# ScalarE instead of SyncE issues the exchange of the transposed exponentials, and VectorE makes two of the output copies

## The chip, the cores and the metric

The kernel runs on one core of a Trainium2 chip. A core has TensorE (PE: matrix products, with its weight load, PEld), VectorE (DVE), ScalarE (ACT), GpSimd (POOL) and SyncE (SP), and 16 DMA engines. The engines run side by side and wait for each other through semaphores. The metric is the time of one execution on the device, in microseconds (us).

## The reference

Three stages follow each other, all in float32.

```python
# 1: attention in chunks of 64 positions, 32 heads-by-batch, head size 64
scores = scale * np.matmul(q_c, k_c.transpose(0, 1, 2, 4, 3))
attn = np.exp(scores - np.max(scores, axis=-1, keepdims=True))
attn = attn / (np.sum(attn, axis=-1, keepdims=True) + 1e-09)
x = np.matmul(attn, v_c)                      # as (2304 tokens, 512)
# 2: eight experts, all of them on every token, weighted by P
P = np.exp(x @ w_gate - max); eight rounds of row and column norms
for e in range(E):
    out += P[:, e:e + 1] * (np.maximum(x @ w1[e], 0.0) @ w2[e])
# 3: a maximum of three products, then one more product
h = np.maximum(np.maximum(x @ w1, x @ w2), x @ w3)
return h @ w_out
```

## The kernel before

The 2304 tokens are 18 tiles of 128, in three blocks of six tiles. An expert has a hidden size of 1024, and a pair of hidden tiles (256 columns) is the unit of the main loop, so an expert is four pairs and all experts are 32 pairs. The loop counter `n` runs over items: 0 to 31 are the pairs of block 0, 32 to 63 those of block 1, 64 to 95 those of block 2, and the rest is stage 3. In this text "pass n" is one turn of this loop.

In each pass `up(n)` computes the pair's hidden values with seven half-size products in place of eight (product positions 0 to 6, line L353). The products of the banks `pa`, `pg` and `pb` build upon each other in PSUM: ScalarE copies the first three to `s` (L360), VectorE adds them to later ones (L366), and the relus (L298) and low parts (L304, L301) follow. The fifth product's sum, `c<-pa`, has to be read out of its bank before product 6 is accumulated into that bank. Between the positions stand the down products of the pair before (`down`, L469), two at each of the positions 1, 3 and 5. They go to two buffers, `dn`, and are taken out by `evict`: for the first pair of an expert by a copy of ScalarE (L482), for the other three by an addition of VectorE (L484, later L488). Since it is the pair before that is evicted, ScalarE does this in the passes 1, 5, 9 and so on.

The values are split in a high part (a cast by ScalarE, L272 in `hilo`, also L159 and L203) and a low part (a subtraction by GpSimd, L273, or VectorE). In block 0 the weights are prepared in the same way while they are used: `prep` and `prep_x` take `sw`, ScalarE copies a part to `xw` in PSUM (L188), VectorE computes four sums from it (L193 to L197), ScalarE casts (L203), VectorE subtracts (L210). `keep` stores the prepared weights for the later blocks (L216 to L223).

The attention of tiles 6 to 17 is spread over the same passes, 1 to 12, one tile each. At position 0 come the scores (`s<-qk`, L804), the gate's product (L922), the value product of the tile before (`xp<-aT,v`, L905, into the `dn` buffers too), the exponentials (L838), at position 1 the norm and VectorE's transposition of 32 by 32 blocks into `eT` (L865), and at position 2 `att_swap`: ScalarE copies `eT` to `aT` (L872), and four transfers of 32 KB inside SBUF then exchange the blocks that have to change partitions (L876). `aT` has two buffers, and `xp` of the next pass reads it.

All engines work through their instructions in the order in which the code above emits them; there is no scheduler that changes it. All transfers are issued by SyncE, in that order too, so that an issue that waits holds up those after it. A transfer tells of its landing by one of a few semaphores.

After block 0's last pair, `y_out` brings its finished tiles into the other layout: four transpositions by TensorE into `yp` (L506), a copy by ScalarE back to `ar` (L508), a store. The last two tiles are done together in pass 34, position 0.

Of the kernel before, what the change touches and what calls it, by code (L numbers as in the profile page):

```python
# [33 lines left out]
NPAIR = E * F // 256  # L34
# [18 lines left out]
def kernel(ctx: ExitStack, tc: tile.TileContext, qk, vv, wg, wts, wts2, out):  # L53
    nc = tc.nc
# [445 lines left out]

    y_due = []

    def y_out(t):
        p = wk.tile([P, KD, P], F32, name="yp", tag="wk")
        for k in range(KD):
            nc.tensor.transpose(p[:, k], ar[:, t, k * P:(k + 1) * P], ident)  # L506
        y = ar[:, t].rearrange("p (k q) -> p k q", k=KD)
        nc.scalar.copy(out=y, in_=p)  # L508
        nc.sync.dma_start(out=ys[t], in_=y)

    def fold_all():
# [270 lines left out]
    def load_qk(t):  # L782
        if t >= NT:
            return
        a = q_t[t] = ap_.tile([P, KD, 2, P], F32, name="qk", tag="qk", bufs=3)
        if t < 3:
            nc.sync.dma_start(out=a[:, 0:2], in_=qk[t, :, 0:2])
            nc.sync.dma_start(out=a[:, 2:4], in_=qk[t, :, 2:4])
        else:
            nc.sync.dma_start(out=a, in_=qk[t])  # L790

    def load_v(t):
        if t < NT:
            v_t[t] = ap_.tile([P, DM], F32, name="v", tag="v", bufs=3)
            nc.sync.dma_start(out=v_t[t], in_=vv[t])
# [72 lines left out]
    def att_swap(t):  # L868
        eT = et_t.pop(t)
        aT = ap_.tile([P, 2, H, 32], F32, name="aT", tag="aT")  # L870
        at_t[t] = aT
        nc.scalar.copy(out=aT, in_=eT)  # L872
        for c in range(2):
            for i in range(2):
                src, dst = 64 * c + 32 * i, 64 * c + 32 * (1 - i)
                nc.sync.dma_start(out=aT[dst:dst + 32, i], in_=eT[src:src + 32, 1 - i])  # L876

    def raw_of(t):
        if t // 2 not in raw_t:
# [124 lines left out]
    for m in range(NT - NPE):  # L1004
        t, n = NPE + m, 1 + m
# [5 lines left out]
    n = NT - NPE + 2  # L1011
# [80 lines left out]
    for k in (4, 5):  # L1092
        for j in range(TS // 2):
            n = first_of[k - 1] + 3 * j
            if k == 4 and j < 2:
                n = first_of[3] + 3 + j
# [17 lines left out]
    with tc.manual_schedule():  # L1114
        nc.vector.memset(wones, 1.0)
        load_qk(0)
        load_qk(1)
        load_v(0)
        load_qk(2)
        raw1(1)  # L1120
        nc.vector.memset(wgr, 0.0)
        nc.vector.memset(ones, 1.0)
        nc.scalar.activation(out=first, in_=ones[:, 0:8], func=AF.Exp)
        make_identity(nc, ident)
        warm(13)
        scores = lambda t: att_qk(t, [head_s(t)[:, g] for g in range(2)])
        scores(0)
        load_qk(3)
        load_v(1)
        part = [plain(j, f)[0] for j in range(3) for f in range(2)]  # L1130
        half_of = lambda i, q: part[i](slice(q, q + 1))
        for k in range(NPE + 2):
            if k == 4:
                half_of(0, 0)
            if k + 1 < NPE:
                warm(4 if k < 4 else 0)
                scores(k + 1)
                if k < 2:
                    load_qk(k + 4)
            if k < NPE:  # L1140
                head_exp(k)
            if k in (1, 2):
                prep(1, k - 1)
            if k >= 5:
                half_of(*((0, 1), (1, 0), (2, 1))[k - 5])
            if k >= 2:
                att_pv(k - 2)
                load_v(k + 1)
            if k == 0:
                load_v(2)  # L1150
            if k == 1:
                raw1(0)
                raw2(0)
                warm(6)
            if k == 4:
                nc.sync.dma_start(out=wgr[:, :, 0:E], in_=wg)
            if k == 5:
                half_of(2, 0)
            if k >= 5:
                load_qk(k + 1)  # L1160
            if 1 <= k <= NPE:
                head_norm(k - 1)
                att_T(k - 1)
            if k == 3:
                xg = x_cols(0, raw_t[0], nc.gpsimd, ap_, xh, xl)
                next(xg)
            if k == 4:
                next(xg)
                next(xg)
            if k == 5:  # L1170
                xg = x_mid(1, raw_t[1])
            if k in (5, 6):
                next(xg)
        part[3]()
        half_of(1, 1)
        part[4]()
        part[5]()
        keep(1, 0)
        raw1(2)
        next(xg)  # L1180
        w2 = w2_first()
        xg = x_last(2, raw_t[2])
        for _ in range(3):
            next(xg)
        next(xg)
        ends = [[plain(j, f)[1:] for f in range(2)] for j in range(3)]
        for j in range(3):
            if j == 2:
                for _ in range(3):
                    next(w2)  # L1190
            for i in range(2):
                for end in ends[j]:
                    end[i]()
        prep_x(0, 0)
        prep_x(0, 1)
        raw2(1)
        prep_sums(2)
        prep_x(0, 2)
        prep_x(0, 3)
        hps.close()  # L1200
        psum = lambda name, n: pool(name, n, space=bass.MemoryType.PSUM, reuse_waits="tile")
        wk, ps_a, dn, ps_g, ps_b = psum("wk", 2), psum("pa", 2), psum("dn", 2), psum("pg", 1), psum("pb", 1)

        pend = [(0, q, j) for q in (1, 0) for j in range(TS // 2)]
        for n in range(1, ni):
            it = items[n]
            big_m = it["kind"] == "m"
            raw1(n + 2)
            for pos in up(n):
                clock[0] = 7 * n + pos  # L1210
                if y_due and y_due[0][0] < 7 * n + pos - 1 and (len(y_due) > 2 or n != NPAIR + 1):
                    y_out(y_due.pop(0)[1])
                    if (n, pos) == (NPAIR + 2, 0):
                        y_out(y_due.pop(0)[1])
                if (n, pos) in early:
                    early[n, pos]()
                if pos in ((2, 4) if n == 1 else (0, 1)):
                    prep(n + 1, pos // 2 - 1 if n == 1 else pos)
                if pos == 2:
                    prep(n, 2)  # L1220
                    prep_x(n, 0)
                elif pos == 5 + (n == 1):
                    prep_x(n, 3)
                for f in bg.get((n, pos), ()):
                    f()
                if (n, pos) != (NPAIR + 1, 6):
                    step()
                if pos < 3:
                    decode_step(n)
                if n <= NPAIR:  # L1230
                    run = 2 if pos in (1, 3, 5) else 0
                else:
                    run = len(pend) if pos == 6 and big_m and it["i"] == 0 else 0
                    if run and n > ni - 4:
                        run = 4
                for i in range(run):
                    if pend:
                        down(*pend.pop(0))
                    while pos == 5 and later:
                        later.pop(0)()  # L1240
                    if n in xcol and n != first_of[3] + 4 and i in (0, 2, 4):
                        next(xcol[n])
                    if (n, i) == (first_of[3] + 3, 3):
                        x_next(4, 1, n + 1)
                if run and big_m and not pend:
                    room(4)
                if pos == 3 + (n == 1):
                    prep_x(n, 1)
                    prep_x(n, 2)
                    raw2(n + 1)  # L1250
            if NPAIR + 2 <= n < first_of[3] + 2:
                for i in half((n - NPAIR) // 2 - 1, n % 2):
                    if n + 1 in first_of[2:4]:
                        if i in (3, 5):
                            x_put((i + 3) // 2, 0)
                    if i in (1, 3):
                        decode_step(n)
                    step()
                while n % 2 == 0 and extras:
                    step()  # L1260
            if n + 1 == first_of[3] + 2:
                while extras:
                    step()
                big_again()
            if it["down"] and (n < NPAIR or big_m):
                assert len(pend) == (2 if n == ni - 1 else 0)
                pend += [(n, q, j) for q in (1, 0) for j in range(TS // 2)]
        while later:
            later.pop(0)()
        for d in pend:  # L1270
            down(*d)
        assert not chunks
# [38 lines left out]
```

## Time and profile before

| | |
|---|---|
| median of 3 runs | 1775.23 us (1775.12 to 1779.2) |
| the profiled execution | 1775.73 us, span 1774.0 us |
| TensorE busy | 1763.7 us (99% of the span) |
| TensorE's weight load busy | 1684.0 us (95%) |
| VectorE busy | 1297.2 us (73%) |
| GpSimd busy | 994.4 us (56%) |
| ScalarE busy | 776.6 us (44%) |
| granted TensorE clock | 1.00 in the whole span (2.4 GHz) |
| DMA | 532.89 MB, mean 300 GB/s, one hardware queue with 83.2% of the engines' span |

The span goes from the first to the last instruction; the execution's own time is a little longer. Busy times don't count register, semaphore and DMA-issuing instructions, so ScalarE's and SyncE's issues are not in them. A row of the timeline has a start, a duration (both us), the engine, the line of the kernel, the operation, out<-in with its shape, and a count where several of a kind are merged; in brackets stand the engine's idle time before it and what ended it. SPq marks SyncE's issues.

### The profile page before, as it was taken

How to read it: one execution, taken by the hardware profiler on the slowest of the kernel's cores; microseconds unless marked ns; L12 is line 12 of the kernel's file. 1: busy time of each engine (PE TensorE's matmuls, PEld its weight loads, DVE VectorE, ACT ScalarE, POOL GpSimd, SP SyncE). 2: the span in 40 equal slices, each digit the busy share in tenths (PEclk: the TensorE clock that was granted, in tenths of full speed). 3: DMA queues.
4: the chain of work that ended last, by engine and by line, in shares of the span. 5: the costliest groups of instructions: out<-in, count | busy, mean ns of one | idle time of the engine just before them, and what ended most of it. 6: DMA issues, size and time to landing. Idle time of an engine off the chain costs nothing.

```text
span 1774.0 us, 30179 instructions
## 1 busy us (share of the span) xinstructions
PE 1763.7 (99%) x10768; PEld 1684.0 (95%) x10768; DVE 1297.2 (73%) x2342; ACT 776.6 (44%) x1566; POOL 994.4 (56%) x891
## 2 busy tenths in 40 slices
PE   9999999999999999999999999999999999999999
PEld 7888888999989999999999999999999999999998
DVE  8767667678876688887886887878787766664535
ACT  6665664655555534343333434434333333323221
POOL 4665665777777766666675677576767555000000
PEclk9999999999999999999999999999999999999999
DMA  8999987899988897988888779888888786877662
GB/s 287 332 349 359 368 322 299 324 374 343 354 306 336 325 321 272 337 298 306 277 316 305 268 256 347 305 297 296 319 301 314 264 306 243 282 258 255 243 245 107
DMA packets 206486, 532.89 MB, mean 300 GB/s; under 512 B 16160, under 2 KB 95360, under 8 KB 181248
## 3 DMA queue, kind: packets, MB, share of 16 engines
q1 hardware_dynamic: 206336, 530.97, 83.2%
q8 instruction: 85, 1.39, 0.3%
q14 instruction: 65, 0.53, 0.1%
HBM read 373.31 MB, written 156.02 MB: 298 GB/s over the span
## 4 chain that ended last, share of the span: by engine, by line
PE 95%; DMA 2%; DVE 1%; ACT 1%; issue 0%; POOL 0%; SPq 0%; DVEq 0%; ACTq 0%; POOLq 0%
PE pa L353 28%; PE dn L411 27%; PE dn L469 18%; PE pg L353 14%; PE pb L353 7%; DMA aT<-eT 1%; DMA upart<-ar 0%; PE xp L905 0%; DMA w2s<-w2y 0%; PE s L804 0%; DMA sw<-in_wts 0%; PE gp L922 0%; PE hq L1112 0%; PE hs L804 0%; DVE e L830 0%
## 5 line engine op out<-in xcount | busy, mean ns | idle before, releaser
L353 PE MATMUL pa<-xh,wr 128*128 128x384 f32 x1808 | 529.6, 337 | 0.7 <-ACT s L360 0.6
L469 PE MATMUL dn<-wr,hr 128*128 128x512 f32 x1476 | 356.2, 392 | 0.0
L353 PEld LDWEIGHTS pa<-xh,wr 128*128 128x128 f32 x1808 | 332.7, 188 | 7.1 <-ACT s L360 1.3
L469 PEld LDWEIGHTS dn<-wr,hr 128*128 128x128 f32 x1476 | 275.4, 188 | 53.9
L353 PE MATMUL pa<-xl,wr 128*128 128x384 f32 x904 | 303.2, 335 | 0.0
L411 PE MATMUL dn<-hr,wr 128*128 128x384 f32 x1344 | 274.7, 335 | 0.0
L353 PE MATMUL pg<-xh,wr 128*128 128x384 f32 x904 | 268.3, 337 | 0.0
L360 ACT COPY s<-pa 128x384 f32<-128x384 f32 x244 | 117.3, 481 | 301.0 <-PE pa L353 278.3
L411 PEld LDWEIGHTS dn<-hr,wr 128*128 128x128 f32 x1344 | 237.0, 188 | 0.0
L366 DVE TENSOR_TENSOR c<-pb,s 128x384 f32<-128x384 f32 x82 | 45.7, 557 | 203.0 <-PE pb L353 179.5
L273 POOL TENSOR_TENSOR hr<-c,hr 128x384 fp32r<-128x384 f32 x96 | 111.0, 1161 | 145.3 <-ACT hr L272 139.0
L411 PE MATMUL dn<-hx,wr 128*128 128x384 f32 x840 | 182.8, 338 | 0.0
L353 PEld LDWEIGHTS pa<-xl,wr 128*128 128x128 f32 x904 | 169.7, 188 | 4.0
L353 PEld LDWEIGHTS pg<-xh,wr 128*128 128x128 f32 x904 | 166.4, 188 | 1.6 <-issue 0.4
L353 PE MATMUL pg<-xl,wr 128*128 128x384 f32 x452 | 151.1, 334 | 0.0
L411 PEld LDWEIGHTS dn<-hx,wr 128*128 128x128 f32 x840 | 150.9, 188 | 0.0
L273 POOL TENSOR_TENSOR hr<-tq,hr 128x384 fp32r<-128x384 f32 x128 | 148.2, 1173 | 0.1
L353 PE MATMUL pb<-xh,wr 128*128 128x384 f32 x452 | 134.1, 337 | 0.0
L420 DVE TENSOR_TENSOR ar<-dn,ar 128x384 f32<-128x384 f32 x240 | 122.9, 546 | 9.3 <-PE dn L411 8.9
L273 POOL TENSOR_TENSOR hx<-c,hx 128x384 fp32r<-128x384 f32 x60 | 68.4, 1143 | 106.5 <-ACT hx L272 106.2
L411 PE MATMUL dn<-hy,wr 128*128 128x384 f32 x504 | 111.1, 336 | 0.0
L420 DVE TENSOR_TENSOR ax<-dn,ax 128x384 f32<-128x384 f32 x180 | 93.1, 549 | 18.5 <-PE dn L411 18.5
(246 smaller groups left out, 3207.7 us busy)
## 6 DMA issues: line engine op xcount, KB each, us to landing
wr<-w2s SPq DMA_DIRECT2D x80, 1024.0 KB, 6.1
w1s<-wr SPq DMA_DIRECT2D x32, 1792.0 KB, 10.5
wr<-w1s SPq DMA_DIRECT2D x53, 1024.0 KB, 8.0
wr<-w1s SPq DMA_DIRECT2D x58, 768.0 KB, 6.9
w2s<-wr SPq DMA_DIRECT2D x55, 512.0 KB, 5.4
wr<-w2s SPq DMA_DIRECT2D x52, 512.0 KB, 7.1
wr<-scr SPq DMA_DIRECT2D x22, 1024.0 KB, 5.1
wr<-scr SPq DMA_DIRECT2D x27, 768.0 KB, 6.1
```

The lines of the kernel that those rows point to most:

```text
L273: (eng or nc.gpsimd).tensor_tensor(out=l, in0=v, in1=h.bitcast(F32), op=ALU.subtract)
L353: nc.tensor.matmul(ps, lhsT=wt[:, x, ws], rhs=y[:, xi, k], start=b not in begun, stop=k == 1 and i == 2, skip_group_check=True)
L360: nc.scalar.copy(out=s[pos], in_=ps)
L366: nc.vector.tensor_tensor(out=inner, in0=ps, in1=s[other], op=ALU.add)
L411: nc.tensor.matmul(p, lhsT=w[:, a, dt * P:(dt + 1) * P], rhs=h[m][:, b], start=m == 0 and q == 0, stop=m == 1 and q == 2)
L420: nc.vector.tensor_tensor(out=o, in0=p, in1=o, op=ALU.add)
L469: nc.tensor.matmul(o, lhsT=h[:, hi, ts], rhs=w, start=(f == 0 and i == 0), stop=(f == 1 and i == 2))
```

## The change

Line L876 is issued by ScalarE's queue instead of SyncE's; the four transfers, their data and their place in the code stay. In pass 34, position 0, the two copies of `y_out` are VectorE's instead of ScalarE's; the other four tiles of block 0 keep ScalarE's copy.

```diff
-    def y_out(t):
+    def y_out(t, copy=nc.scalar.copy):
...
-        nc.scalar.copy(out=y, in_=p)
+        copy(out=y, in_=p)
         nc.sync.dma_start(out=ys[t], in_=y)
...
                 src, dst = 64 * c + 32 * i, 64 * c + 32 * (1 - i)
-                nc.sync.dma_start(out=aT[dst:dst + 32, i], in_=eT[src:src + 32, 1 - i])
+                nc.scalar.dma_start(out=aT[dst:dst + 32, i], in_=eT[src:src + 32, 1 - i])
...
                 if y_due and y_due[0][0] < 7 * n + pos - 1 and (len(y_due) > 2 or n != NPAIR + 1):
-                    y_out(y_due.pop(0)[1])
-                    if (n, pos) == (NPAIR + 2, 0):
-                        y_out(y_due.pop(0)[1])
+                    last = (n, pos) == (NPAIR + 2, 0)
+                    for _ in range(1 + last):
+                        y_out(y_due.pop(0)[1], nc.vector.tensor_copy if last else nc.scalar.copy)
```

## Rows read from the trace of the kernel before

**Rows 1.** Part 1 of the page: busy us (share of span) xinstructions.

```profile
PE 1763.7 (99%) x10768; PEld 1684.0 (95%) x10768; DVE 1297.2 (73%) x2342; ACT 776.6 (44%) x1566; POOL 994.4 (56%) x891
```

**Rows 2.** TensorE's waits over the span: us in total, times, longest.

```profile
PE xp L905 <- DMA aT<-eT: 0.8, 1, 0.8
```

**Rows 3.** Stretches: length, then busy us by engine, clock, DMA share, GB/s.

```profile
124.00:141.00 17.00, 16.08 (x114) 14.18 (x107) 12.84 (x29) 9.14 (x21) 9.37 (x9) 1.00 0.99 348
...
192.00:210.00 18.00, 17.57 (x158) 15.30 (x157) 12.27 (x28) 10.66 (x25) 10.40 (x10) 1.00 0.94 346
```

**Rows 4.** The tile aT: durations in ns min/median/max; its transfers' time to landing.

```profile
L876 SPq DMA_DIRECT2D aT<-eT x48: 507/718/1372, 44.8 to 239.8; - x48
...
DMA to landing us min/median/max: 2.8/6.5/11.3
```

**Rows 5.** Timeline of SyncE's issues, 36 to 250 us: the exchange.

```profile
44.76 2.73 SPq L876 DMA_DIRECT2D aT<-eT  x4
...
60.50 3.50 SPq L876 DMA_DIRECT2D aT<-eT  x4
...
167.44 4.85 SPq L876 DMA_DIRECT2D aT<-eT  x4
...
184.15 3.84 SPq L876 DMA_DIRECT2D aT<-eT  x4
...
202.61 4.56 SPq L876 DMA_DIRECT2D aT<-eT  x4
...
219.74 2.41 SPq L876 DMA_DIRECT2D aT<-eT  x4
```

**Rows 6.** Timeline of pass 1, 42.6 to 53 us.

```profile
42.65 0.62 ACT L872 COPY aT<-eT 128x512 f32<-128x512 f32 x1 [0.79 <-DVE eT L865]
...
43.18 0.83 ACT L272 CAST wr<-st 128x768 fp32r<-128x768 f32 x1
...
46.05 1.06 ACT L482 COPY ar<-dn 128x512 f32<-128x512 f32 x2
...
47.02 2.92 PE L469 MATMUL dn<-wr,hr 128*128 128x512 f32 x12
...
52.46 0.69 PE L804 MATMUL s<-qk 64*64 64x64 f32 x30 [0.16 <-DVE wr L210]
```

**Rows 7.** Timeline of pass 2, 60 to 68.5 us.

```profile
61.41 0.79 ACT L188 COPY xw<-sw 128x256 f32<-128x256 f32 x2
...
64.02 0.68 DVE L193 TENSOR_TENSOR wr<-xw,wr 128x512 fp32r<-128x512 f32 x1
...
66.20 0.55 DVE L366 TENSOR_TENSOR c<-pa,s 128x384 f32<-128x384 f32 x1
...
68.08 0.33 PE L353 MATMUL pa<-xh,wr 128*128 128x384 f32 x1
```

**Rows 8.** Timeline of pass 5, 110 to 128 us.

```profile
109.07 1.25 SPq L790 DMA_DIRECT2D qk<-in_qk  x1
...
113.39 3.87 SPq L876 DMA_DIRECT2D aT<-eT  x4
...
115.28 0.58 ACT L482 COPY ar<-dn 128x512 f32<-128x512 f32 x1
...
117.95 2.92 PE L469 MATMUL dn<-wr,hr 128*128 128x512 f32 x12
```

**Rows 9.** SyncE's waits, 184 to 189 us; the page's issues: KB, us to landing.

```profile
SPq L876 <- DMA qk<-in_qk: 1.1, 1, 1.1
...
qk<-in_qk SPq DMA_DIRECT2D x15, 512.0 KB, 6.7
```

**Rows 10.** Timeline of pass 34, 574 to 580 us.

```profile
575.18 1.08 ACT L508 COPY ar<-yp 128x512 f32<-128x512 f32 x2
...
578.42 0.56 DVE L366 TENSOR_TENSOR c<-pb,s 128x384 f32<-128x384 f32 x1 [1.38 <-PE pb L353]
...
578.71 0.44 PE L353 MATMUL pa<-xh,wr 128*128 128x384 f32 x1 [0.42 <-ACT s L360]
```

## The prediction

> **What bounds the kernel now.** I read the page first. TensorE is busy 1763.7 us of a span of 1774.0 us [rows 1], so in the whole program it stands idle 10.3 us. A change that only takes waits away cannot gain more than that. Then I read TensorE's list of waits and the table of stretches. The wait that the change aims at is there: the value product `xp<-aT,v` waits for the exchange `aT<-eT` once, for 0.8 us [rows 2], in the stretch from 124 to 141 us, where TensorE is idle for 0.92 us; from 192 to 210 us it loses another 0.43 us ahead of the same product [rows 3]. A third wait, of `pa` for the copy `s`, takes 0.42 us at 578.71 us [rows 10], where the two moved copies are. TensorE's other waits lie in the first 21 us, but for two of 0.2 us.
>
> So the gain has a ceiling of about 1.8 us (0.92 + 0.43 + 0.42), a tenth of a per cent. The question is what ScalarE's new work costs.
>
> **The issue moves to ScalarE.** There are 12 exchanges of 4 transfers, in passes 1 to 12 of the pair loop, with 48 issues of 0.51 to 1.37 us (median 0.72 us), landing 2.8 to 11.3 us later [rows 4]. SyncE spends 2.41 to 4.85 us on the four [rows 5], six rows of the 12. In the order of the code they now stand on ScalarE between the copy L872 and the casts L159 and L272 (in pass 1 the cast L272). ScalarE starts its next instruction 0.53 us after L872 begins, 0.09 us before L872 ends [rows 6]; now it must let L872 end, issue four transfers, and start again. Hence everything behind is late by the four issues plus some 0.2 us.
>
> What do four issues cost on ScalarE? The trace has none there, so I bound them by SyncE's. The lower end is nothing per issue. The nearest undisturbed row is pass 11, where the four take 2.41 us [rows 5]; the long ones come where large transfers of the same queue are still in flight, and ScalarE's queue would hold nothing else. I take 2.4 us, so a lateness of 2.6 us. The upper end is 4.85 + 0.2 = 5.05 us.
>
> One more thing can hold ScalarE. In pass 9 the four took 3.84 us because one waited 1.1 us for the load `qk` to land [rows 5, 9], which has nothing to do with `aT`: the semaphores that tell of a landing are used again in turn, and an issue waits until the earlier transfer on its semaphore is in. If ScalarE's issues take part in that turn, ScalarE stands still for it. In pass 5 the `qk` load leaves at 109.07 us [rows 8] and such a load needs 6.7 us [rows 9], so the last issue could not end before some 116.5 us: lateness 3.3 us. In pass 9 it is 4.0 us, in pass 1 about 2.9 us.
>
> **Who waits for the late ScalarE.** Queued behind the issues are the casts, the copies `xw` L188, the relu L298 and, in some passes, the eviction of the down product. I looked for each consumer's slack.
>
> In passes 2 to 4, 6 to 8 and 10 to 12 the evictions are VectorE's. There the chain is L188, then VectorE's L193 to L197, then L366 `c<-pa`, which frees the bank that TensorE wants at product 6. L188 ends at 62.20 us and VectorE comes to L193 at 64.02: 1.8 us of slack. L366 ends at 66.75 and TensorE begins product 6 at 68.08: 1.3 us more [rows 7]. A lateness up to 3.1 us costs nothing; mine is 2.6. Nine passes at 0.
>
> In passes 1, 5 and 9 the pair before is the first of its expert and ScalarE itself evicts `dn` (L482). There are two `dn` buffers. In pass 5 the first eviction ends at 115.86 us and TensorE wants that buffer at 117.95 [rows 8]: slack 2.1 us; pass 9 has the same pattern 70.89 us later. With lateness 2.6 us each loses 0.5 us, with the semaphores' turn 1.2 and 1.9 us.
>
> Pass 1 is the worst. ScalarE has no gap there: the first L482 is done at about 46.6 us and TensorE wants the buffer at 47.02; at the end of the pass TensorE waits 0.16 us for L210, which ends the chain through ScalarE [rows 6]. The lateness goes through nearly whole: 2.6 to 2.9 us.
>
> **What it gives back.** The exchange no longer stands behind SyncE's bulk transfers, and the two waits ahead of `xp`, 0.92 and 0.43 us [rows 3], should go: four transfers of 32 KB on a queue of their own have to land only by the next pass. The Trainium skill's DMA: Bandwidth & Descriptors (Queues, rings and completion order) says that SyncE and ScalarE each own a row of rings and that a DMA engine takes turns between rows; by that the 1.3 us are regained.
>
> SyncE is freed of a wait too: the store `xs<-xr` leaves earlier. The next, the load of `sw`, waits for VectorE anyway. I count nothing.
>
> **Two copies to VectorE.** At 575.18 us ScalarE copies two outputs in 1.08 us, and TensorE then waits 0.42 us for a late `s` at 578.71 us. VectorE has 1.38 us idle before 578.42 us [rows 10]. Two copies at ScalarE's rate fit. At half that rate (2.2 us) VectorE would be 0.8 us late. I take a gain of 0.4 us; the ends are a gain of 0.42 and a loss of 0.8 us.
>
> **The sum.** Without the semaphores' turn: 2.6 + 0.5 + 0.5 − 0.92 − 0.43 − 0.4 = +1.9 us. With it: 2.9 + 1.2 + 1.9 − 0.92 − 0.43 − 0.4 = +4.3 us. The trace shows the turn, so I lean to the second, but the loss in pass 1 gives the transfers time to catch up: +4.0 us. The profiled execution took 1775.73 us (span 1774.0 and 1.7 around it) and would take 1779.7; it lies 0.5 us above the median of 1775.23, so I forecast 1779.2 us. That is 0.23%, under the 0.3% (5.3 us) that a measurement can tell from no change.
>
> **Rivals.**
>
> *ScalarE's issues are as long as SyncE's.* Then lateness follows the 12 rows of SyncE plus 0.2 us. Of the nine easy passes three have 4.56 to 4.85 us, 1.6 to 1.9 us above the slack, 5.3 us together; the other six have 2.41 to 3.50 us [rows 5] and give some 1.1 us. Pass 1 gives 2.9, passes 5 (3.87 us [rows 8]) and 9 some 1.9 each, less 1.75 of gains: +12 us, 1787 us. It decides from a lateness of 3.1 us on, at product 6 of the VectorE passes. For it: every issue after the first in a group is longer where bulk is in flight. Against it: the other queue would be nearly empty. By the Trainium skill's Perfetto Trace Analysis (DMA Instruction — HWDGE (DVE, Sync)) the recorded issue includes a wait for a generator locked for one user at a time; that would speak for this rival. Chance 0.27.
>
> *An issue on ScalarE costs next to nothing.* Lateness is some 0.5 us: pass 1 loses 0.5 to 0.7, the rest none, and the gains stay: −1 us, 1774.2 us. Against it is that no issue on SyncE is below 0.5 us. Chance 0.13.
>
> *The exchange lands no sooner on ScalarE's queue,* so the change doesn't do what it is made for: the 1.35 us are not regained, +5.4 us, 1780.6 us. By the Trainium skill's DMA: Bandwidth & Descriptors (Issuing engines are not separate DMA queues) it would be so: all issuers share the same DMA engines, and a second one saves only the time of issuing. For it: the DMA engines are 0.99 busy from 124 to 141 us [rows 3]. Against it: 32 KB needed 2.8 us at best and 11.3 us at worst [rows 4], so most of the long landings is time spent behind other transfers of the queue. Chance 0.07.
>
> *Faster by over 5.3 us.* It would need half of all of TensorE's idle time, most of it outside these passes. Chance 0.03.
>
> **How the numbers follow.** My forecast has 0.50, with its own range of 1777 to 1780.5 us; about a tenth of it lies above 1780.6. Slower by over 0.3%: 0.24 of the first rival, 0.05 of the forecast, half of the third: 0.33. Faster 0.03. The same 0.64. The range goes from 1774 (the cheap issue) to 1787 us.
>
> **What would show it.** Right: idle TensorE of 2 to 3 us at about 47 us, released by ScalarE's L482; some of it at 118 and 189 us; no wait for `aT<-eT`; landings well below 6.5 us; no new idle time before product 6 in the other passes; the wait at 578 us gone. Wrong: issues on ScalarE under 0.2 us or over 0.8 us each, or a wait ahead of L876 on ScalarE in many passes. The forecast fails most easily at the length of an issue, which I took from another engine.

## The result, and the profile after

The changed kernel takes 1795.8 us (median of 5 runs, 1793.81 to 1798.96) against 1775.23 us before (5 runs, 1774.67 to 1779.2): a ratio of 1.0115, interval 1.0099 to 1.0131. It is 20.6 us slower, well outside the forecast range. The profiled execution took 1793.81 us with a span of 1792.0 us, 18.0 us more than before; the account below is of these 18.0 us, and what the other runs have beyond them is not split up.

First, the page's busy times, which answer to [rows 1]:

```profile
PE 1767.8 (99%) x10768; PEld 1685.7 (94%) x10768; DVE 1298.3 (72%) x2344; ACT 776.0 (43%) x1564; POOL 994.9 (56%) x891
```

TensorE has the same instructions and is busy 4.1 us longer, so some of them ran slower. The other 13.9 us are idle time. TensorE's list of waits of the changed kernel (us in total, times, longest) says where:

```profile
PE pa L353 <- DVE c L366: 8.3, 7, 2.2
PE dn L469 <- ACT ar L482: 4.2, 3, 2.3
PE pa L353 <- ACT s L360: 1.9, 2, 1.6
...
PE xp L905 <- DVE ar L484: 0.6, 1, 0.6
```

Before, neither of the first two was in the list. They are the two places for which the prediction had worked out a slack: product 6 behind `c`, and the `dn` buffer behind ScalarE's eviction. The wait of `xp` for `aT<-eT` [rows 2] is gone. Adding all of TensorE's idle time in passes 1 to 12 gives 13.5 us (8.3 + 4.2 + some 1.0 ahead of `xp`) where it was 1.5: +12.0. Pass 34 gives +1.2, the first 35 us, ahead of any changed line, +0.8, and busy time +4.1; together 18.1.

The exchange itself, the tile `aT` (durations in ns, min/median/max; time to landing), answers to [rows 4]; ACTq marks ScalarE's issues:

```profile
L876 ACTq DMA_DIRECT2D aT<-eT x48: 514/804/1762, 43.7 to 256.9; - x48
...
DMA to landing us min/median/max: 3.0/5.4/7.0
```

It lands earlier, as hoped: 7.0 us at the worst, not 11.3. But an issue on ScalarE is no shorter than it was on SyncE. The four of a pass take 2.45 to 5.08 us, 3.62 us in the mean; SyncE's took 3.56, SyncE's waits between the four included. ScalarE's list of waits from 40 to 265 us shows that time as idle ("issue" here is the four issues ahead of the cast):

```profile
ACT wr L159 <- issue: 32.0, 8, 5.2
```

Pass 7 is the worst. The chain of waits from 155 to 166 us (start, length, what) leads from the copy L872 through the issues to TensorE:

```profile
154.69 0.63 ACT aT L872
...
155.34 0.51 ACTq L876
...
155.89 1.34 ACTq L876
...
157.27 1.34 ACTq L876
...
158.66 1.76 ACTq L876
...
160.46 0.62 ACT wr L159
...
161.91 0.39 ACT xw L188
...
164.51 0.56 DVE c L366
...
165.12 1.01 PE pa L353 x2
```

L159 starts 5.77 us after L872 began, where 0.53 was usual [rows 6], so ScalarE is 5.2 us late; with 3.1 us of slack 2.1 us are left. The timeline shows 2.17, and beside it a row of pass 1:

```profile
49.77 3.00 PE L469 MATMUL dn<-wr,hr 128*128 128x512 f32 x12 [2.33 <-ACT ar L482]
...
165.12 0.69 PE L353 MATMUL pa<-xh,wr 128*128 128x384 f32 x1 [2.17 <-DVE c L366]
```

The last row holds a second loss: that product takes 0.69 us where 0.33 is usual. The table of stretches has the granted clock in the column before the last two:

```profile
160.00:164.00 4.00, 2.94 (x14) 2.09 (x12) 1.65 (x4) 2.21 (x5) 1.29 (x1) 1.00 0.48 179
...
166.00:168.00 2.00, 2.00 (x8) 2.00 (x7) 2.00 (x4) 1.54 (x4) 2.00 (x2) 0.50 0.83 247
...
227.00:229.00 2.00, 2.00 (x36) 1.56 (x39) 1.77 (x4) 0.97 (x3) 1.92 (x4) 0.50 1.02 347
```

TensorE had stood idle for 2.17 us, and in pass 10, ending at 225.1 us, for 1.89 us. After each the clock was at its lower level, 0.50 (1.2 GHz), for 3.4 us. Half of these 6.8 us is 3.4 us of the 4.1; the rest I could not place. The wait of 2.33 us in pass 1 was not followed by it (twelve products in 3.00 us; 2.92 before).

Pass 34, where VectorE makes the two copies (timeline, all engines):

```profile
593.36 1.28 DVE L508 COPY ar<-yp 128x512 f32<-128x512 f32 x2
594.56 1.26 DVE L322 TENSOR_TENSOR tq<-c 128x384 f32<-128x384 f32 x1
...
595.85 0.51 ACT L272 CAST hr<-tq 128x384 fp32r<-128x384 f32 x1 [1.58 <-DVE tq L322]
596.27 0.47 ACT L360 COPY s<-pg 128x384 f32<-128x384 f32 x1
...
598.08 0.45 PE L353 MATMUL pa<-xh,wr 128*128 128x384 f32 x1 [1.65 <-ACT s L360]
```

The copies fit VectorE's load but not its order: they stand ahead of the subtraction L322, ScalarE's cast waits for that, the copy `s` stands behind the cast, and TensorE waits 1.65 us where it waited 0.42 [rows 10].

### The profile page after: what moved, and what is told of

It reads as the page before. It is cut to its first block, busy times and chain, and to the rows that moved or that the text cites. A ratio compares the mean times of both kernels' runs of the same rounds, so it can differ in the third digit from the quotient of the medians.

```text
span 1792.0 us, 30161 instructions
## 1 busy us (share of the span) xinstructions
PE 1767.8 (99%) x10768; PEld 1685.7 (94%) x10768; DVE 1298.3 (72%) x2344; ACT 776.0 (43%) x1564; POOL 994.9 (56%) x891
## 3 DMA queue, kind: packets, MB, share of 16 engines
HBM read 373.31 MB, written 156.02 MB: 295 GB/s over the span
## 4 chain that ended last, share of the span: by engine, by line
PE 91%; DVE 2%; ACTq 2%; ACT 2%; issue 2%; DMA 1%; POOL 0%; SPq 0%; DVEq 0%; POOLq 0%
PE pa L353 27%; PE dn L411 26%; PE dn L469 16%; PE pg L353 13%; PE pb L353 6%; ACTq L876 2%; PE xp L905 0%; PE hs L660 0%; ACT aT L872 0%; ACT wr L159 0%; ACT wr L272 0%; ACT xw L188 0%; DMA v<-in_v 0%; DMA aT<-eT 0%; PE s L804 0%
## 6 DMA issues: line engine op xcount, KB each, us to landing
w1s<-wr SPq DMA_DIRECT2D x32, 1792.0 KB, 10.2
```

## The experiments

The theory after these rows: ScalarE is late by its four issues, and each pass loses what exceeds its slack. Rival causes: the lateness of something else that moved (SyncE's stores, the landing), the two copies, or an issue that is long because the two engines disturb each other.

**The exchange alone**, with the copies left on ScalarE.

```diff
-                nc.sync.dma_start(out=aT[dst:dst + 32, i], in_=eT[src:src + 32, 1 - i])
+                nc.scalar.dma_start(out=aT[dst:dst + 32, i], in_=eT[src:src + 32, 1 - i])
```

> The changed kernel with the two output copies back on ScalarE. If the issue of the exchange on ScalarE is the cause: +17 to +20 us over the kernel before, TensorE's waits in passes 1 to 12 as in the changed kernel, and the wait for `s` in pass 34 back from 1.65 to 0.4 us. If the two copies are the cause: within 2 us of the kernel before.

1794.12 us beside 1775.73: ratio 1.0101, 1.0087 to 1.0114. TensorE's waits:

```profile
PE pa L353 <- DVE c L366: 9.6, 8, 2.1
PE dn L469 <- ACT ar L482: 4.2, 3, 2.6
```

So nearly all of the loss, 18.4 us, is the exchange's.

**The copies alone.**

```diff
-                    y_out(y_due.pop(0)[1])
-                    if (n, pos) == (NPAIR + 2, 0):
-                        y_out(y_due.pop(0)[1])
+                    last = (n, pos) == (NPAIR + 2, 0)
+                    for _ in range(1 + last):
+                        y_out(y_due.pop(0)[1], nc.vector.tensor_copy if last else nc.scalar.copy)
```

> The kernel before with only the two output copies on VectorE. If the exchange is the cause: +1 to +1.5 us, all of it in pass 34, where the wait for `s` grows from 0.42 to some 1.6 us. If the copies are the cause: +17 us or more.

1776.74 us: ratio 1.0006, 0.9997 to 1.0014. The time can't tell it from before, but the list of waits repeats the row of the changed kernel:

```profile
PE pa L353 <- ACT s L360: 1.8, 2, 1.6
```

**ScalarE late, the exchange on SyncE.** If lateness is the cause, dummy work in the place of the issues must bring the same waits, with no transfer on ScalarE's queue.

```diff
-    pool("edge", side="right").tile([P, 120], F32, name="edge")
+    edge = pool("edge", side="right").tile([P, 120], F32, name="edge")
...
+        for _ in range(20):
+            nc.scalar.copy(out=edge, in_=ident[:, 0:120])
```

> The kernel before (SyncE issues the exchange), with 20 small copies on ScalarE behind each L872 that nobody reads: ScalarE is late by some 3 to 4 us, as by the four issues, while queues and semaphores stay as they were. If ScalarE's lateness alone is the cause: about 3 us in pass 1, 0.5 to 1 us ahead of product 6 in each of the nine VectorE passes, 1 to 2 us in passes 5 and 9: +9 to +16 us. If the second queue and the changed order of SyncE's transfers are the cause: 0 to +3 us.

1843.7 us: ratio 1.0389, 1.0373 to 1.0405. The copies were longer than I had estimated; ScalarE's timeline in pass 2, and TensorE's waits:

```profile
68.77 6.45 ACT L878 COPY edge<-ident 128x120 f32<-128x120 f32 x20
75.13 0.62 ACT L159 CAST wr<-sw 128x512 fp32r<-128x512 f32 x1
```

```profile
PE pa L353 <- DVE c L366: 28.5, 9, 3.3
PE dn L469 <- ACT ar L482: 14.2, 3, 6.0
```

L159 is 6.4 us late. Nine passes wait for `c` 3.2 us each, which makes the slack 3.2 us. Pass 1 waits 6.0 us and the passes 5 and 9 share 8.2, 4.1 each: slacks of 0.4 and 2.3. The same two places and no others, so lateness of ScalarE alone is enough. TensorE is busy 1785.1 us, 21 us longer; its granted clock is 0.50 after ten of these twelve waits.

**The same with 11 copies**, 3.5 us, near the mean length of the four issues.

```diff
+        for _ in range(11):
+            nc.scalar.copy(out=edge, in_=ident[:, 0:120])
```

> As e3_scalar_late with 11 copies instead of 20: by the 0.318 us that each took there, ScalarE is 3.5 us late in every pass, about the mean of the four issues on ScalarE (3.6 us). SyncE issues. If lateness beyond each pass's slack is the whole cause: 0.4 us ahead of product 6 in each of the nine VectorE passes, 1.4 us in passes 5 and 9, 3 us in pass 1: 9 us of waits, +8 to +12 us with what the clock adds; less than the changed kernel, whose issues are uneven. If the changed kernel loses by something else too: +8 us all the same here, and the difference stays open.

1788.84 us beside 1775.46: ratio 1.0078, 1.0063 to 1.0093.

```profile
PE dn L469 <- ACT ar L482: 5.6, 3, 3.1
PE pa L353 <- DVE c L366: 2.2, 9, 0.4
```

Nine waits of 0.24 us: 3.5 less 3.2, again. An even lateness of 3.5 us costs 13.4 us, more than the 8 to 12 expected: 7.8 us are these waits, and TensorE is busy 1769.0 us, 5.3 us longer than before. The exchange alone has 13.8 us of these two waits. Most of that difference is a larger mean: its four issues take 3.70 us, with the 0.2 us a lateness of 3.9. By the slacks of 3.2, 0.4 and 2.3 us an even lateness of 3.9 us would give 13.0 us. Only the last 0.8 us are left for the unevenness: what exceeds the slack counts, and what falls short gives nothing back.

**The issues later in ScalarE's order**, behind the copies L188 and the evictions, ahead of L203.

```diff
+        swaps.append((aT, eT))
...
                 if pos == 3 + (n == 1):
+                    att_issue()
                     prep_x(n, 1)
```

> ScalarE issues the exchange, but behind L188 and the eviction of position 3, just ahead of L203, where ScalarE waits some 2.5 to 3.7 us for VectorE anyway; output copies on ScalarE. If the lateness of what stands behind the issues is the cause: the waits for L482 and `c` go, +0 to +5 us (pass 1 has no gap on ScalarE, and `xp` may wait for a later landing). If the second queue itself is the cause: +15 us or more, as in the changed kernel.

1778.95 us: ratio 1.0018, 1.0008 to 1.0027. The issues (L884 in this kernel, 514/602/1382 ns) are somewhat shorter, the four 3.07 us in the mean. But in passes 4, 5, 8 and 9 they take 3.75 to 3.92 us, more than the slacks at the old place, and yet no wait for `c` or for L482 is left (`xp` is L913 here):

```profile
187.41 3.87 ACTq L884 DMA_DIRECT2D aT<-eT  x4
```

```profile
PE xp L913 <- DMA aT<-eT: 1.9, 2, 1.5
PE s L804 <- DVE wr L210: 0.7, 1, 0.7
```

The place of the issues in ScalarE's order decides, not that ScalarE issues them. The price is that the exchange starts later and `xp` waits for it.

**The large store earlier.** Why are issues long on a queue that holds nothing else? SyncE's 1.8 MB store `w1s<-wr` (L216) was still in flight in most passes of the changed kernel (KB each, median us to landing):

```profile
w1s<-wr SPq DMA_DIRECT2D x32, 1792.0 KB, 10.2
```

Here it leaves at position 4 of the pass before, with the exchange on ScalarE, and in a control with the exchange on SyncE.

```diff
-                at(g + a if g or s_ else NPAIR, b, lambda g=g, s_=s_: keep(g if g or s_ else NPAIR, s_))
+                n_, b = (g - 1, 4) if 3 <= g <= 13 and not s_ else (g + a if g or s_ else NPAIR, b)
+                at(n_, b, lambda g=g, s_=s_: keep(g if g or s_ else NPAIR, s_))
```

> ScalarE issues the exchange at its place (output copies on ScalarE); the store of the 1.8 MB of prepared weights (w1s) leaves at position 4 of the pass before, for pairs 3 to 13, instead of at position 0. If the issues are long because this store's transfer is in flight right ahead of them: the four take 2.4 to 2.8 us in passes 3 to 12, the waits for `c` go, and +4 to +8 us are left over the kernel before. If they are long for another reason (a generator shared with SyncE's issues): 3.6 us on average and +15 us or more.

> Control of e6_store_earlier: the kernel before (SyncE issues the exchange) with the same earlier store. Either theory: within 2 us of the kernel before; its two waits of 1.3 us for the exchange may go, or SyncE may stand still for GpSimd.

With ScalarE 1787.89 us (ratio 1.0076, 1.006 to 1.0092), the control 1781.11 us (1.0031, 1.0019 to 1.0043). The control was to stay within 2 us and did not: the early store makes `s<-qk` wait for L210 (3.8 us) and `xp` for L482 (2.5 us). Against its own control the exchange on ScalarE now costs 6.8 us, not 18.4. ScalarE's issues and TensorE's waits, exchange on ScalarE:

```profile
83.50 2.44 ACTq L876 DMA_DIRECT2D aT<-eT  x4
...
101.32 2.44 ACTq L876 DMA_DIRECT2D aT<-eT  x4
...
247.84 3.08 ACTq L876 DMA_DIRECT2D aT<-eT  x4
```

```profile
PE dn L469 <- ACT ar L482: 3.8, 3, 2.5
...
PE pa L353 <- DVE c L366: 0.8, 1, 0.8
```

In passes 3 to 12 the four now take 2.44 to 3.08 us, 2.67 in the mean, where the exchange-alone kernel has 3.84; five of the ten passes have 2.44 or 2.45 us, near the value that the prediction took. The waits for `c` fall from 9.6 us to 0.8. The one that remains is in pass 2, whose store is not moved and whose issues still take 3.87 us. So ScalarE's issues are long mainly where that store is in flight on SyncE's queue. Two things keep this from being exact. The earlier store shifts SyncE's other transfers too, and the passes 5 and 11 have become longer (2.72 to 2.99 us, 2.45 to 2.90 us). And 4 to 8 us over the kernel before were expected, where 12.4 were measured; 5.7 of these are the control's.

**Two issues on each engine.**

```diff
-                nc.scalar.dma_start(out=aT[dst:dst + 32, i], in_=eT[src:src + 32, 1 - i])
+                (nc.sync if c else nc.scalar).dma_start(out=aT[dst:dst + 32, i], in_=eT[src:src + 32, 1 - i])
```

> ScalarE issues two of the four transfers, SyncE the other two; output copies on ScalarE. If the lateness against the slack decides: 1.3 to 2 us late, below the slack of 3.1 us (VectorE passes) and 2.1 us (passes 5 and 9), 1 to 1.5 us lost in pass 1 only: 0 to +3 us. If any use of the second queue costs in proportion: half of the loss, +9 us.

1775.59 us beside 1775.46: ratio 1.0003, 0.9993 to 1.0013. ScalarE's two take 1.4 to 2.0 us in the passes, under the slacks of 3.2 and 2.3 us:

```profile
PE xp L905 <- DMA aT<-eT: 1.4, 1, 1.4
PE dn L469 <- ACT ar L482: 1.0, 1, 1.0
```

The one wait for L482 left is pass 1's, which has almost no slack.

**The same with pass 1 all on SyncE.**

```diff
-                nc.scalar.dma_start(out=aT[dst:dst + 32, i], in_=eT[src:src + 32, 1 - i])
+                (nc.sync if c or t == NPE else nc.scalar).dma_start(out=aT[dst:dst + 32, i], in_=eT[src:src + 32, 1 - i])
```

> As e8_two_of_four, but in pass 1, the only one without slack, SyncE issues all four. If slack decides: the 1.0 us of waiting for L482 in pass 1 goes, -1 to 0 us against the kernel before, which five rounds can hardly tell from no change. If not: the same as e8_two_of_four or above it.

1775.65 us beside 1775.53: ratio 0.9998, 0.9989 to 1.0007. The wait for L482 is gone; the wait for the exchange is not:

```profile
PE xp L905 <- DMA aT<-eT: 1.2, 1, 1.2
```

No version tried beats the kernel before by more than can be measured.

## Why the prediction was wrong

**The step that failed** is the length of the four issues: "the long ones come where large transfers of the same queue are still in flight, and ScalarE's queue would hold nothing else. I take 2.4 us, so a lateness of 2.6 us." The queue does not protect them. They took 3.62 us in the mean, up to 5.08, and the forecast stood just under a slack of 3.1 us, so most of the error turned into waits. This is the first rival (12 us, chance 0.27; its terms as written add up to 11.4). Its mechanism and its place came true, and so did its amount for passes 1 to 12 taken together, +12.0 us of idle time. Pass by pass the amount did not: SyncE's rows, which it went by, have 4.79 us in pass 4 and 3.25 in pass 7, where ScalarE took 3.79 and 5.08. So the agreement of the two sums is in part luck.

**The slacks were right.** Here is the prediction's own rule, lateness = four issues + 0.2, less 3.1 us (0 in pass 1, 2.1 in passes 5 and 9), fed with the measured lengths. The column of the store says when `w1s<-wr` left against the first of the four issues.

| pass | four issues, us | store left | by the rule | TensorE's wait |
|---|---|---|---|---|
| 1 | 2.54 | none near | 2.7 | 2.33 |
| 2 | 3.09 | 4.7 before | 0.2 | 0 |
| 3 | 3.59 | 4.7 before | 0.7 | 0.55 |
| 4 | 3.79 | 4.7 before | 0.9 | 0.75 |
| 5 | 2.74 | 2.6 after | 0.8 | 0.71 |
| 6 | 3.83 | 0.3 after | 0.9 | 0.79 |
| 7 | 5.08 | 0.3 before | 2.2 | 2.17 |
| 8 | 4.62 | 2.1 before | 1.7 | 1.57 |
| 9 | 3.19 | 4.3 after | 1.3 | 1.16 |
| 10 | 4.93 | 1.4 before | 2.0 | 1.89 |
| 11 | 2.45 | 5.3 before | 0 | 0 |
| 12 | 3.57 | 5.9 before | 0.7 | 0.53 |

The rule gives 14.1 us and the rows 12.5. The longest issues are those with the store just ahead of them. The passes 11 and 12 do not fit that order: the store left 5.3 and 5.9 us ahead and was still in flight in both, and the four took 2.45 and 3.57 us. The columns come from rows of this kind (timelines of SyncE and ScalarE, changed kernel):

```profile
155.01 0.33 SPq L216 DMA_DIRECT2D w1s<-wr  x1
155.34 5.08 ACTq L876 DMA_DIRECT2D aT<-eT  x4
...
196.37 3.19 ACTq L876 DMA_DIRECT2D aT<-eT  x4
200.63 0.33 SPq L216 DMA_DIRECT2D w1s<-wr  x1
```

**The semaphores' turn** was expected to hold ScalarE, for 1.2 and 1.9 us in the passes 5 and 9. ScalarE never waited for it. SyncE did, which the prediction had counted at nothing. Its waits from 40 to 265 us:

```profile
SPq L911 <- DMA aT<-eT: 14.8, 3, 8.2
...
SPq L216 <- DMA qk<-in_qk: 9.1, 4, 2.7
```

Before, L911 waited 0.9 us in all and L216 not at all; SyncE's time went into waiting for ScalarE ahead of the exchange. The store L911 does not read what the exchange writes, so I read the first row as the turn; that was not tried. What such waits do can be seen in pass 7: the store of 1.8 MB left 4.7 us ahead of the exchange before, and 0.3 us ahead of it now, after a wait of 2.7 us for `qk`. SyncE's rows of pass 7 before:

```profile
144.67 0.69 SPq L216 DMA_DIRECT2D w1s<-wr  x1
149.34 3.25 SPq L876 DMA_DIRECT2D aT<-eT  x4
```

So the move makes the very transfer that lengthens the issues coincide with them in that pass.

**The gains.** The waits for `aT<-eT` went as predicted, 1.3 us, so the third rival fell. The Trainium skill's DMA: Bandwidth & Descriptors (Issuing engines are not separate DMA queues) says that transfers of all issuers interleave on the same DMA engines, and that a second issuer saves only issuing time, usually small. Here the longest landing fell from 11.3 to 7.0 us, so more than that was saved, while the issuing time cost 18.4 us with what follows from it.

**The two copies** were put at a gain of 0.4 us with a worst case of a loss of 0.8. The rate was near the one taken (0.64 us each, 0.54 on ScalarE). The loss was 1.2 us because I had looked at VectorE's idle time and not at the subtraction L322 behind the copies, which ScalarE and then TensorE wait for.

**The clock** was no term of the sum. Two waits of about 2 us were each followed by 3.4 us at half clock, and TensorE was busy 4.1 us longer in all.

## What to carry to other kernels

An issue on a compute engine is an instruction in that engine's order: give it the length that such issues have on the engine they come from, long ones included, and put it where the engine's consumers have that much slack, or spread the issues until each share fits. A slack is used up pass by pass, so forecast with the rows of every pass and not with a typical one. Where lateness comes within a few tenths of a slack, as 2.6 against 3.1 did here, the longer case deserves the larger chance.

## What was not expected of the hardware

An issue of 32 KB took 0.51 us at the least and up to 1.76 us on a queue that is all but empty. The page's queues (packets, MB, share of 16 engines) list it:

```profile
q10 hardware_dynamic: 2304, 1.58, 0.3%
```

It was not SyncE's issuing that held it. In pass 7 SyncE's timeline has these neighbours:

```profile
155.69 0.33 SPq L911 DMA_DIRECT2D xs<-xr  x1
164.73 0.38 SPq L124 DMA_DIRECT2D sw<-in_wts  x1
```

SyncE issued nothing from 156.02 to 164.73 us, while three of ScalarE's issues took 1.34, 1.34 and 1.76 us; only the first of them had begun before, by 0.13 us. The Trainium skill's Perfetto Trace Analysis (DMA Instruction — HWDGE (DVE, Sync)) counts a wait for a generator used by one issuer at a time into a recorded issue. These rows show long issues with no other issuer recorded at that time; the first of each four, closest to the copy L872, never took more than 0.60 us. How a transfer in flight slows an issue on another queue stays open.
